# A three-stage float32 kernel on one TensorE: other PSUM banks for half of an output phase, a later place for operand preparation, and another slot for weight conversions

## The chip, the cores and the metric

The kernel runs on one core of a Trainium2 chip. The metric is the time of one execution on the device in microseconds (us). The core's engines work side by side, each through its own list of instructions in order: TensorE (PE in the profile: matrix products into the PSUM banks), VectorE (DVE: arithmetic on tiles), ScalarE (ACT: copies, casts, activation functions) and SyncE (SP: it issues the transfers of the DMA queues). An instruction that needs another engine's result waits for it, and everything behind it on its engine waits too.

## What is computed

The reference, cut to what matters:

```
# attention over a window of 64 positions, 4 batches x 8 heads, 576 positions, head size 64
mask = (rel >= 0) & (rel < 64);  attn = softmax(where(mask, q @ k.T / 8, -1e9)) @ v
x = attn.transpose(0, 2, 1, 3).reshape(2304, 512)
# gated MLP, d_ff = 1536
xn = x / sqrt(mean(x * x, axis=-1) + 1e-6) * rms_g
x2 = (silu(xn @ w_gate) * (xn @ w_val)) @ w_out
# second MLP, d_ff = 2048
h = x2 @ w_in
out = (h * sigmoid(1.702 * h)) @ w_out2
```

All is float32. The kernel gets float32 accuracy from three fast products: an operand is split into a high part (rounded to the fast matmul format) and a low part (the remainder), and high x high, low x high and high x low are summed in PSUM. In the code these are the pairs `xh`/`xl`, `ah`/`al`, `whi`/`wlo`.

## The kernel before

The 2304 tokens are columns of the matmuls, features are the partitions. There are eight PSUM banks: four accumulators with the tags `acc0` to `acc3`, two with the tags `g` and `v`, and a pool `atp` of two with the tag `att`. There are three passes.

**Pass one** (to about 366 us of the span) takes six blocks `j` of 384 tokens through the first half of the gated MLP's features, six chunks `f` of 128. One chunk is 36 matmuls of 128x384: twelve into `psg` (L95, the gate), twelve into `psv` (the value), and twelve of `emit_O` that add the chunk before into the four `acc` banks. ACT takes a function of the gate (L803), DVE multiplies (L806, L810), ACT and DVE split the result into `ah` and `al` (L813, L814). Between the matmuls of block `j` the attention of block `j+1` is worked off, pinned in program order on PE: scores `ps_s` (32 small matmuls), their mask and row maximum on DVE (eight L380 for a group of 128 tokens), the exponentials on ACT (L392), the sums, transposes (`ps_t`), and `ps_v`, the product with v. The scores of one group fill one bank of four tiles; `ps_v` is put into a bank of the same pool and so comes after L380s that read it. At the end of the last chunk of a block `split_x` makes the next block's `xh` (ACT L494 and DVE L492, two each) and `xl` (four L496 on DVE) from the scaled attention output; the next block's first `psg` needs `xh`, its ninth to twelfth matmul need `xl`.

**Weight conversions.** The weights come in another 32-bit format and are converted by `w_step`: two passes on ACT (L230, L231), a shift and an addition on DVE (L232, L237). For pass two a conversion is finished by the next `w_step` call, which runs `w_products`: four additions on DVE (L172 to L175), the high part on ACT (L180) and the low part on DVE (L181, 128x1792), and two stores to DRAM. In pass one a conversion is called from `extras(f, i)`, three slots per chunk, with `s = 3 * f + i`. In the blocks after the first it is called where `s % 9 == 8`: twice in a block, after `f=2` and after `f=5`, the latter at the end of the block. Conversions for pass two go on until block 3.

**Operand preparation.** Pass two multiplies by a scheme of seven products in place of eight (on halves of tokens and features), whose operands `xop` are sums and differences of the input tiles `xr`, split in high and low. `x_steps` returns seven steps for a superblock: a sum on DVE (L661, in four of them), the high part on ACT (L663), the low part on DVE (L664). For the first superblock the steps are called in the last block of pass one, one after chunk 1 and two after each later chunk, and they are needed when pass two begins.

**Pass two** (366 to 587 us) is the second half of the gated MLP's features, in three superblocks of 768 tokens. Each has six chains of seven products (`psa`, `psb`; even chains in the banks `g` and `v`, odd ones in the two `att` banks) and then an output phase, `out_units`. This is made of two halves, `t=1` and then `t=0` (384 tokens each). A half is four units of twelve matmuls (three per accumulator) and four closing pieces `last(t, c)` of six matmuls, 72 in all. A closing piece is followed by L919 on DVE, which adds the partial result of pass one (loaded by L918) to the accumulator `c`, and by a store (L920). Both halves use `acc0` to `acc3`, so a first matmul of `t=0` into `acc` number `c` waits for the L919 of `t=1` with that `c`. The closing pieces of `t=0` are spread over the first chain of the next superblock. On DVE the last seven `xop` steps for the next superblock, a weight conversion and the products `g` (L880, L883) lie around that place.

**Pass three** (587 us to the end) is the second MLP with the same product scheme for `w_in` and plain products for `w_out2`.

The order on the engines is made by the code order, by a scheduler that moves instructions by their readiness, by `keep_in_program_order` on PE, and by `issue_after`, which puts an instruction behind a given one.

Of the kernel before, what the change touches and what calls it, by code (L numbers as in the profile page):

```python
# [8 lines left out]
F32 = mybir.dt.float32  # L9
# [4 lines left out]
ALU = mybir.AluOpType  # L14
# [8 lines left out]
def window_attention__gated_mlp__mlp_kernel(  # L23
# [13 lines left out]
    nc = tc.nc  # L37
# [4 lines left out]
    KC = DM // 128  # L42
# [21 lines left out]
    acc_p = ctx.enter_context(tc.tile_pool(name="acc", bufs=1, space=PSUM))  # L64
# [4 lines left out]
    atp = ctx.enter_context(tc.tile_pool(name="atp", bufs=2, space=PSUM))  # L69
# [87 lines left out]
    def after(ins):  # L157
        return tc.issue_after(ins) if ins is not None else nullcontext()
# [326 lines left out]
    def rms_scale(x, sq, lo, hi, s4=None):  # L485
        rms_sum(x, sq, lo, hi, s4)
        return rms_spread(x, lo, hi)

    def split_x(x, xh, xl, T):
        for c in range(KC):  # L490
            if c % 2:
                nc.vector.tensor_copy(xh[:, c, :T], x[:, c, :T])  # L492
            else:
                last = nc.scalar.copy(xh[:, c, :T], x[:, c, :T]).ins  # L494
        for c in range(KC):
            nc.vector.tensor_tensor(xl[:, c, :T], x[:, c, :T], xh[:, c, :T].bitcast(F32), ALU.subtract)  # L496
        return last

    def proj(ps, w, xh, xl, T):
# [16 lines left out]
    xd = {}  # L516
# [54 lines left out]
    for m in range(2 * m0, N_ATT):  # L571
        b, i = divmod(m, m0)
        t, n = score_at[m - 2 * m0], score_at[m - 2 * m0 + 1] - score_at[m - 2 * m0]
# [13 lines left out]
    if True:  # L587
# [27 lines left out]
        x, sq = x_of(0)  # L615
# [21 lines left out]
        T = TB  # L637
# [8 lines left out]
        def x_raws(src):  # L646
            r = [wp.tile([128, KC, TB], F32, tag="w", name="xr") for _ in range(2)]
            for e in range(2):
                nc.sync.dma_start(out=r[e], in_=src(e))
            return r  # L650

        def x_steps(r, ops):
            a11, a12, a21, a22 = r[0][:, 0:2, :], r[0][:, 2:4, :], r[1][:, 0:2, :], r[1][:, 2:4, :]
            subs = [
                (0, None, a11), (6, (a21, a11, a21, ALU.subtract), a21), (5, (a21, a22, a21, ALU.subtract), a21),
                (4, (a11, a11, a21, ALU.add), a11), (2, (a21, a12, a21, ALU.subtract), a21), (1, None, a12), (3, None, a22),
            ]

            def step(i, total, src):
                if total:  # L660
                    nc.vector.tensor_tensor(*total)  # L661
                t = x1p.tile([128, 2, 2, TB], F32R, tag="xop", name="xop")
                nc.scalar.copy(t[:, 0], src)  # L663
                nc.vector.tensor_tensor(t[:, 1], src, t[:, 0].bitcast(F32), ALU.subtract)  # L664
                ops[i] = t

            return [lambda a=a: step(*a) for a in subs]
# [100 lines left out]
        for j in range(NB):  # L768
# [17 lines left out]
            def extras(f, i):  # L786
                s = 3 * f + i
                for fn in slots.pop(j * NS + s, ()):
                    fn()
                if j == 0:  # L790
                    if s % 2 == 0:
                        w_step(n_wh)
                elif s % 9 == 8:
                    w_step(n_w1)

            pend = None
            for f in range(FH):
# [17 lines left out]
                if f == FH - 1 and not end:  # L815
                    nxh = xp.tile([128, KC, TB], F32R, tag="x", name="xh")
                    nxl = xp.tile([128, KC, TB], F32R, tag="x", name="xl")
                    x = xs.pop(j + 1)[0]
# [12 lines left out]
                if f == 0 and end:  # L831
                    at_es.close()
                    x1p = ctx.enter_context(tc.tile_pool(name="x1p", bufs=7))
                    ops = {}
                    todo = x_steps(x_raws(lambda e: xd[e]), ops)
                if f == 4 and end:
                    loads(0, 2)
                if f >= 1 and end:
# [54 lines left out]
        def out_units(sb, g):  # L893
# [13 lines left out]

            def unit(t, k):
                if k == 0:
                    accs[t] = [acc_p.tile([128, 512], F32, tag=f"acc{c}", name="acc") for c in range(KC)]  # L910
                for c in range(KC):
                    mms(t, *order[k], c)

# [280 lines left out]
```

## Time and profile before

| what | value |
|---|---|
| time, median of 3 runs (lowest, highest) | 953.79 us (949.55, 954.65) |
| profiled execution: its time | 956.72 us |
| its span | 954.9 us |
| PE busy | 919.3 us, 96% |
| DVE busy | 605.9 us, 63% |
| ACT busy | 512.1 us, 54% |
| mean granted TensorE clock | 0.979 of full speed |

The span is the profiled execution from its first to its last instruction; 1.8 us of the time lie around it. Busy is the time in which an engine had an instruction under way. Matmuls overlap, so that a train of 128x384 ones starts one every 0.174 us where each has a duration of about 0.34 us; the end of a train therefore hangs over the next start by about 0.17 us, and the idle time that a row gives is shorter than the delay of the start by about that much. "Issue" as a releaser is a wait for which the profile shows no releasing instruction.

### The profile page before, as it was taken

Reading aid. Unit: us, or ns where it says so; the run is one execution under the profiler, and the core shown is the slowest. Engines: PE = TensorE matmul, PEld = TensorE weight load, DVE = VectorE, ACT = ScalarE, POOL = GpSimd, SP = SyncE. Lnnn points to the kernel's source line nnn. Section 1 sums busy time; section 2 is a strip of 40 time slices with the busy share of each in tenths; the row PEclk is TensorE's granted clock in tenths of the full one; section 3 lists DMA queues with packets and bytes.
Section 4 is the critical chain, followed back from the end, with each engine's and each line's share of the span. In section 5 each row is a group of like instructions: output and inputs, shape, how many; then the busy total and the mean of one; then the engine's idle time right before and its main releaser. Section 6 shows DMA issues by size and latency. Waiting matters only on the chain.

```text
span 954.9 us, 16476 instructions
## 1 busy us (share of the span) xinstructions
PE 919.3 (96%) x6398; PEld 880.5 (92%) x6398; DVE 605.9 (63%) x1216; ACT 512.1 (54%) x1028; POOL 12.1 (1%) x39
## 2 busy tenths in 40 slices
PE   8889899999989899989999999999999999999998
PEld 7888798998989899979999999988989999999998
DVE  5798477667774725892892787656563469334753
ACT  7796475655653416742651664665554555345442
POOL 2000000000000000000000000000000000000000
PEclk9899799999999999989998999999999999999999
DMA  9865555675753274977976999988667778867861
GB/s 224 228 181 169 132 143 169 179 210 186 210 160 140 104 276 156 340 267 263 370 274 209 336 366 323 332 279 325 233 244 281 272 301 282 297 216 273 321 226 50
DMA packets 153646, 227.96 MB, mean 239 GB/s; under 512 B 80608, under 2 KB 130784, under 8 KB 149984
## 3 DMA queue, kind: packets, MB, share of 16 engines
q1 hardware_dynamic: 153040, 226.91, 71.1%
q8 instruction: 50, 0.82, 0.3%
q14 instruction: 28, 0.23, 0.1%
q10 hardware_dynamic: 528, 0.00, 0.0%
HBM read 167.64 MB, written 59.24 MB: 238 GB/s over the span
## 4 chain that ended last, share of the span: by engine, by line
PE 74%; DVE 12%; ACT 5%; DMA 5%; issue 3%; SPq 0%; POOL 0%; DVEq 0%; ACTq 0%
PE acc L95 17%; PE psa L95 14%; PE psb L95 11%; PE psg L95 7%; PE psv L95 7%; PE acca L95 6%; PE accb L95 5%; DVE xop L664 2%; PE ps_v L95 2%; PE ps_s L95 2%; PE ps_t L95 1%; DMA xr<-x 1%; ACT st L231 1%; DMA st<-in_moe_w_in_dram 1%; DVE xr L661 1%
## 5 line engine op out<-in xcount | busy, mean ns | idle before, releaser
L95 PE MATMUL psa<-xop,wt 128*128 128x384 f32 x1008 | 192.9, 335 | 0.4 <-DMA wt<-wv 0.4
L95 PEld LDWEIGHTS psa<-xop,wt 128*128 128x128 f32 x1008 | 176.6, 188 | 3.3 <-DMA wt<-wv 0.8
L95 PE MATMUL psb<-xop,wt 128*128 128x384 f32 x756 | 147.1, 335 | 0.8 <-DVE sn L704 0.8
L95 PEld LDWEIGHTS psb<-xop,wt 128*128 128x128 f32 x756 | 132.6, 188 | 3.3 <-DVE sn L704 1.1
L704 DVE TENSOR_TENSOR sn<-sn,psb 128x384 f32<-128x384 f32 x84 | 46.3, 552 | 80.5 <-PE psb L95 79.6
L95 PE MATMUL acc<-g,w 128*128 128x384 f32 x432 | 87.5, 356 | 6.2 <-DVE part L919 5.9
L95 PEld LDWEIGHTS acc<-g,w 128*128 128x128 f32 x432 | 80.9, 202 | 9.9 <-DVE part L919 9.2
L95 PE MATMUL psg<-xh,w 128*128 128x384 f32 x288 | 68.5, 363 | 4.6 <-ACT xh L494 2.6
L95 PE MATMUL acca<-wo,sop 128*128 128x256 f32 x576 | 72.0, 283 | 0.2 <-DVE sop L1002 0.2
L1002 DVE TENSOR_TENSOR sop<-g,sop 128x768 fp32r<-128x768 f32 x56 | 53.3, 957 | 28.6 <-ACT sop L1001 28.5
L95 PEld LDWEIGHTS acca<-wo,sop 128*128 128x128 f32 x576 | 70.8, 191 | 0.5 <-DVE sop L1002 0.5
L700 ACT COPY sn<-psa 128x384 f32<-128x384 f32 x84 | 40.0, 476 | 57.3 <-PE psa L95 57.3
L1001 ACT CAST sop<-g 128x768 fp32r<-128x768 f32 x56 | 46.4, 835 | 40.5 <-PE accb L95 23.2
L95 PE MATMUL acc<-whi,g 128*128 128x512 f32 x192 | 67.8, 392 | 0.0
L392 ACT ACTIVATE p<-p,sm 128x128 f32<-128x128 f32 x128 | 49.6, 389 | 22.2 <-DVE sm L380 22.1
L95 PE MATMUL psv<-xh,w 128*128 128x384 f32 x288 | 61.2, 344 | 0.0
L95 PEld LDWEIGHTS psg<-xh,w 128*128 128x128 f32 x288 | 51.5, 198 | 8.3 <-ACT xh L494 3.6
L95 PE MATMUL acc<-ah,w 128*128 128x384 f32 x288 | 58.9, 340 | 0.0
L978 ACT ACTIVATE g<-sn 128x384 f32<-128x384 f32 x48 | 25.2, 526 | 52.3 <-DVE sn L704 52.3
L95 PE MATMUL accb<-wo,sop 128*128 128x256 f32 x432 | 52.8, 283 | 0.0
L95 PEld LDWEIGHTS accb<-wo,sop 128*128 128x128 f32 x432 | 52.3, 192 | 0.0
L95 PEld LDWEIGHTS psv<-xh,w 128*128 128x128 f32 x288 | 50.8, 191 | 0.4 <-issue 0.2
(135 smaller groups left out, 1514.8 us busy)
## 6 DMA issues: line engine op xcount, KB each, us to landing
wt<-wh SPq DMA_DIRECT2D x48, 896.0 KB, 6.4
wo<-wp SPq DMA_DIRECT2D x28, 1024.0 KB, 6.1
st<-in_moe_w_out_dram SPq DMA_DIRECT2D x28, 512.0 KB, 7.8
wt<-wg SPq DMA_DIRECT2D x14, 896.0 KB, 6.6
wt<-wv SPq DMA_DIRECT2D x14, 896.0 KB, 8.0
xr<-x SPq DMA_DIRECT2D x12, 768.0 KB, 7.3
wh<-whi SPq DMA_DIRECT2D x8, 896.0 KB, 8.3
wh<-m SPq DMA_DIRECT2D x8, 896.0 KB, 8.6
```

The source lines that it names most:

```text
L95: ins = op(*args, **kw)
L231: nc.scalar.activation(lo, lo.bitcast(U32), AF.Copy, scale=2.0 ** -29)
L392: last_exp[0] = nc.scalar.activation(p[e][:, hp, :], p[e][:, hp, :], AF.Exp, bias=sm[:, 0, i:i + 1], scale=-1.0, accum_out=sm[:, 1, i:i + ...
L661: nc.vector.tensor_tensor(*total)
L664: nc.vector.tensor_tensor(t[:, 1], src, t[:, 0].bitcast(F32), ALU.subtract)
L700: nc.scalar.copy(t, ps[:, :TB])
L704: nc.vector.tensor_tensor(t, t, ps[:, :TB], ALU.add)
L978: hold[0] = nc.scalar.activation(g[pg, q][:, j % 2], c, AF.Gelu_apprx_sigmoid).ins
L1001: nc.scalar.copy(t[:, 0], src)
L1002: nc.vector.tensor_tensor(t[:, 1], src, t[:, 0].bitcast(F32), ALU.subtract)
```

## The change

The change has three parts. (1) In `out_units` the four accumulators of `t=0` are now two `att` banks and `acc0`, `acc1`, in this order; `t=1` keeps `acc0` to `acc3`. (2) The steps of `x_steps` for the first superblock get `hold_on=split_end`: each instruction of a step is put behind the last L496 of the latest `split_x` on the same engine. That is an order on DVE alone, where the L496 stands. (3) The conversions in the blocks after the first are called at `s % 9 == 4`, in the middle of chunks 1 and 4 (behind the value's products, `i=1`), instead of at the end of chunks 2 and 5.

```
     def split_x(x, xh, xl, T):
...
         for c in range(KC):
-            nc.vector.tensor_tensor(xl[:, c, :T], x[:, c, :T], xh[:, c, :T].bitcast(F32), ALU.subtract)
+            low = nc.vector.tensor_tensor(xl[:, c, :T], x[:, c, :T], xh[:, c, :T].bitcast(F32), ALU.subtract).ins
+        split_end[0] = low
         return last
...
-        def x_steps(r, ops):
+        def x_steps(r, ops, hold_on=()):
...
             def step(i, total, src):
+                with ExitStack() as es:
+                    for ins in hold_on:
+                        es.enter_context(after(ins))
+                    make(i, total, src)
+
+            def make(i, total, src):
                 if total:
                     nc.vector.tensor_tensor(*total)
...
-                elif s % 9 == 8:
+                elif s % 9 == 4:
                     w_step(n_w1)
...
-                    todo = x_steps(x_raws(lambda e: xd[e]), ops)
+                    todo = x_steps(x_raws(lambda e: xd[e]), ops, split_end)
...
             def unit(t, k):
                 if k == 0:
-                    accs[t] = [acc_p.tile([128, 512], F32, tag=f"acc{c}", name="acc") for c in range(KC)]
+                    tags = ("acc0", "acc1", "acc2", "acc3") if t else ("att", "att", "acc0", "acc1")
+                    accs[t] = [
+                        (atp if tag == "att" else acc_p).tile([128, 512], F32, tag=tag, name="acc") for tag in tags
+                    ]
```

The order of the instructions on PE is the same in both kernels; the waits differ. On PE at the first superblock's output phase, where the half `t=0` begins, there stood before (acc_4604 is the last accumulator of `t=1`, acc_4751 to acc_4754 are those of `t=0` for `c` = 0 to 3, the name in brackets is the semaphore that is waited for):

```order
L95 MATMUL acc_4604<-g_4625,w_4426 128x384 x3
L95 MATMUL acc_4751<-g_4330,w_4250 128x384 [waits DVE_49]
L95 MATMUL acc_4751<-g_4330,w_4250 128x384 x2
L95 MATMUL acc_4752<-g_4330,w_4250 128x384 [waits DVE_49]
L95 MATMUL acc_4752<-g_4330,w_4250 128x384 x2
L95 MATMUL acc_4753<-g_4330,w_4250 128x384 [waits DVE_49]
L95 MATMUL acc_4753<-g_4330,w_4250 128x384 x2
L95 MATMUL acc_4754<-g_4330,w_4250 128x384 [waits DVE_49]
L95 MATMUL acc_4754<-g_4330,w_4250 128x384 x2
```

and in the changed kernel, at the same place on PE:

```order
L95 MATMUL acc_4604<-g_4625,w_4426 128x384 x3
L95 MATMUL acc_4751<-g_4330,w_4250 128x384 x3
L95 MATMUL acc_4752<-g_4330,w_4250 128x384 x3
L95 MATMUL acc_4753<-g_4330,w_4250 128x384 [waits DVE_49]
L95 MATMUL acc_4753<-g_4330,w_4250 128x384 x2
L95 MATMUL acc_4754<-g_4330,w_4250 128x384 [waits DVE_49]
L95 MATMUL acc_4754<-g_4330,w_4250 128x384 x2
```

The first two accumulators have no wait any more, and the last two wait for the L919 of the first two accumulators of `t=1`.

On DVE around the `split_x` for the last block of pass one (L492 and L496; L661 and L664 are the operand preparation) there stood before:

```order
L661 TENSOR_TENSOR xr<-xr 128x768
L810 TENSOR_TENSOR a<-a,psv 128x384
L661 TENSOR_TENSOR xr<-xr 128x768
L664 TENSOR_TENSOR xop<-xr,xop 128x768
L814 TENSOR_TENSOR al<-a,ah 128x384
L492 CAST xh<-xraw 128x384 x2
L496 TENSOR_TENSOR xl<-xraw,xh 128x384 x2
L661 TENSOR_TENSOR xr<-xr 128x768
L664 TENSOR_TENSOR xop<-xr,xop 128x768
L496 TENSOR_TENSOR xl<-xraw,xh 128x384 x2
```

and in the changed kernel (its line numbers are higher by 2 in `split_x` and by 9 behind it):

```order
L819 TENSOR_TENSOR a<-a,psv 128x384
L823 TENSOR_TENSOR al<-a,ah 128x384
L494 CAST xh<-xraw 128x384 x2
L498 TENSOR_TENSOR xl<-xraw,xh 128x384 x4
L673 TENSOR_TENSOR xop<-xr,xop 128x768
L670 TENSOR_TENSOR xr<-xr 128x768
```

All of the preparation on DVE now stands behind the split, whose four L498 follow each other.

On DVE in block 1 of pass one, ahead of the L380s of one of its score groups, there stood before:

```order
L453 TENSOR_TENSOR sq<-s_1699 128x128
L814 TENSOR_TENSOR al<-a,ah 128x384
L806 SCALAR_TENSOR_TENSOR a<-a,psg 128x384
L380 ISA p,sm<-ps_s,masks 128x128
L380 ISA sm 128x1
```

and in the changed kernel:

```order
L453 TENSOR_TENSOR sq<-s_1699 128x128
L823 TENSOR_TENSOR al<-a,ah 128x384
L815 SCALAR_TENSOR_TENSOR a<-a,psg 128x384
L232 TENSOR_SCALAR m<-st 128x1024
L237 ISA m<-st,m 128x2048
L380 ISA p,sm<-ps_s,masks 128x128
L380 ISA sm 128x1
```

The second conversion of this block, which stood at its end, now has its shift and addition ahead of these L380s.

## Rows read from the trace of the kernel before

**Rows 1.** The page's first part: busy time, share of the span, instructions.

```profile
PE 919.3 (96%) x6398; PEld 880.5 (92%) x6398; DVE 605.9 (63%) x1216; ACT 512.1 (54%) x1028; POOL 12.1 (1%) x39
```

**Rows 2.** PE's waits: what waited for whom, us in total, times, longest.

```profile
PE acc L95 <- DVE part L919: 5.9, 6, 1.8
PE ps_v L95 <- issue: 5.5, 4, 2.6
```

**Rows 3.** Timeline, PE, first superblock's output phase: start, us, instruction, [idle before <- releaser].

```profile
414.80 7.06 PE L95 MATMUL acc<-g,w 128*128 128x384 f32 x36
423.68 1.01 PE L95 MATMUL acc<-g,w 128*128 128x384 f32 x3 [1.82 <-DVE part L919]
425.08 2.66 PE L95 MATMUL acc<-g,w 128*128 128x384 f32 x6 [0.39 <-DVE part L919]
428.62 9.65 PE L95 MATMUL acc<-g,w 128*128 128x384 f32 x39 [0.87 <-DVE part L919]
```

**Rows 4.** Timeline, DVE, the same stretch.

```profile
416.54 0.55 DVE L880 TENSOR_TENSOR a<-a,psa 128x384 f32<-128x384 f32 x1
...
423.07 0.55 DVE L919 TENSOR_TENSOR part<-part,acc 128x384 f32<-128x384 f32 x1
```

**Rows 5.** Timeline, PE, second superblock's output phase.

```profile
500.16 1.72 PE L95 MATMUL acc<-g,w 128*128 128x384 f32 x6 [1.05 <-DVE part L919]
503.29 9.82 PE L95 MATMUL acc<-g,w 128*128 128x384 f32 x39 [1.41 <-DVE part L919]
```

**Rows 6.** Windows: stretch, length, busy times of PE to POOL, granted clock, DMA share, GB/s.

```profile
219.27:222.69 3.42, 3.37 (x37) 3.19 (x38) 2.84 (x14) 3.42 (x15) 0.00 (x0) 0.50 0.10 24
424.07:434.31 10.24, 8.98 (x27) 7.45 (x26) 7.95 (x13) 1.69 (x1) 0.00 (x0) 0.50 1.00 344
502.58:509.41 6.83, 6.12 (x19) 6.12 (x20) 1.53 (x3) 0.00 (x0) 0.00 (x0) 0.50 0.88 283
```

**Rows 7.** Timeline, PE, pass one: stalls at the starts of blocks 2 to 5.

```profile
161.60 0.44 PE L95 MATMUL psg<-xh,w 128*128 128x384 f32 x1 [1.38 <-ACT xh L494]
...
164.30 0.45 PE L95 MATMUL psg<-xl,w 128*128 128x384 f32 x1 [0.32 <-DVE xl L496]
...
219.32 1.98 PE L95 MATMUL ps_v<-pt,qkv 128*64 128x64 f32 x32 [2.21 <-issue]
...
275.36 1.15 PE L95 MATMUL ps_v<-pt,qkv 128*64 128x64 f32 x32 [2.56 <-issue]
...
323.05 1.49 PE L95 MATMUL psg<-xh,w 128*128 128x384 f32 x7 [0.81 <-DVE xh L492]
...
326.45 0.91 PE L95 MATMUL psg<-xl,w 128*128 128x384 f32 x3 [1.75 <-DVE xl L496]
```

**Rows 8.** Timeline, DVE, inside the last `split_x` of pass one.

```profile
324.11 0.95 DVE L661 TENSOR_TENSOR xr<-xr 128x768 f32<-128x768 f32 x1
```

**Rows 9.** Instruction groups by line and shape: count, busy us, mean ns, idle before.

```profile
L237 DVE CUSTOM_DVE_ANT_0 m<-st,m 128x2048 uint16<-128x2048 uint16 x34 | 41.5, 1221 | 3.5 <-ACT st L231 2.8
L231 ACT ACTIVATE st<-st 128x1024 int32<-128x1024 uint32 x34 | 39.3, 1155 | 0.0
L181 DVE TENSOR_TENSOR m<-m,whi 128x1792 fp32r<-128x1792 f32 x14 | 28.3, 2023 | 4.6 <-ACT whi L180 4.4
L230 ACT ACTIVATE st<-st 128x1024 f32<-128x1024 f32 x25 | 28.2, 1130 | 3.2 <-DMA st<-in_moe_w_in_dram 2.4 <-DMA st<-in_moe_w_out_dram 0.9
L232 DVE TENSOR_SCALAR m<-st 128x1024 uint32<-128x1024 uint32 x34 | 23.5, 692 | 16.7 <-ACT st L230 15.8 <-DMA qkv<-in_q_dram 0.5 <-ACT st L228 0.4
L172 DVE TENSOR_TENSOR m<-m 128x256 f32<-128x256 f32 x22 | 9.2, 419 | 0.0
```

**Rows 10.** Timelines, block 1: ACT's gate function, a score group's L380s, the `ps_v` behind.

```profile
144.22 0.49 ACT L803 ACTIVATE a<-psg 128x384 f32<-128x384 f32 x1 [1.47 <-PE psg L95]
...
145.96 0.29 DVE L380 CUSTOM_DVE_ANT_0 p<-ps_s,masks 128x128 f32<-128x128 f32 x1 [0.67 <-PE ps_s L95]
...
147.78 1.15 PE L95 MATMUL ps_v<-pt,qkv 128*64 128x64 f32 x32
```

More of the change, by code (lines that the diff above doesn't have):

```diff
@@ L487, in rms_scale @@
         return rms_spread(x, lo, hi)
+    split_end = [None]
     def split_x(x, xh, xl, T):
```

## The prediction

> **What bounds the kernel now.** First the busy times: TensorE is busy for 96% of the span, the next engine for 63% [rows 1]. So a change counts only where it lets TensorE start earlier or run faster, and what there is to win lies in its stalls and in stretches at half clock. Second its waits by releaser: the largest is on L919, the evictions of the output phase, with 5.9 us in six waits, and the next a wait of `ps_v` without a named releaser, 5.5 us in four [rows 2]. The places of both, read next in the timelines, are where this change works: the middle of the output phases [rows 3, 5] and the starts of the blocks of pass one [rows 7]. Third the granted clock: 2.4 GHz nearly everywhere, but at the lower level, 1.2 GHz (0.50), for 10.24 us behind the first stall of L919, for 6.83 us around the second, and for 3.42 us from the `ps_v` stall at 219.32 [rows 6]. It did not fall at every stall: at 275.36 TensorE had idled 2.56 us, and the 32 matmuls of `ps_v` behind took 1.15 us, against 1.98 at 219.32 [rows 7]. The pitch of a 128x384 matmul at full clock is 0.174 us (39 of them take 6.79), and a stall delays the next start by about 0.2 us more than its idle time, since a train hangs over.
>
> **Part 1, other banks.** In the first superblock the half `t=1` ends with 36 matmuls from 414.80 that last 7.06 us; less the overhang of 0.17 the next could start at 421.69. The first one of `t=0` starts at 423.68, its second accumulator at 425.08, its fourth at 428.62, each behind an L919 [rows 3]. The L919 themselves are late because VectorE works off its list in order: the first starts at 423.07 [rows 4], although its accumulator was complete before. The change does not move these evictions. But now `c`=0 and 1 go to the `att` banks, last read by L880 at 416.54 [rows 4], and so run at once, from 421.69 to 422.73. `c`=2 takes the bank of the first L919 and starts at 423.68 as `c`=0 did (a delay of 0.95), `c`=3 that of the second, and starts at 425.08 in place of 428.62. Then 39 matmuls without a wait follow; they took until 428.62 + 9.65 less 0.17 = 438.10, for the most part at half clock [rows 3, 6]. At full clock they end at 425.08 + 6.79 = 431.87: **6.2 us earlier**, 3.5 of it from the start and 2.7 from the clock.
>
> In the second superblock the stalls are at 500.16 and 503.29 [rows 5]; the release that `c`=3 now needs is the one that let `c`=1 go at 500.16. So 500.16 + 6.79 = 506.95, against 503.29 + 9.82 less 0.17 = 512.94: **6.0 us**. In the third superblock there is one short wait, 5.9 less the five shown (5.54) [rows 2, 3, 5], below 0.4. In the order of the changed kernel two `wlo` conversions of VectorE lie ahead of all four L919 there, so that I count nothing. Costs: the first `att` bank is wanted again by the next superblock's second chain, which starts only when the first chain and the closing pieces of `t=0` between its products are over, and `c`=0 is evicted first among these; I count nothing, and at most one L919 of 0.55 [rows 4] per superblock if that fails.
>
> **Part 2, preparation held.** At the last block's start TensorE waits 0.81 for an `xh` of VectorE and 1.75 for an `xl` [rows 7]; inside the split stands an L661 (324.11, 0.95 us) [rows 8], with an L664 of like length behind it, and more of both lie close ahead. With all of these behind the split the four `xl` follow each other and both waits go: 0.81 + 1.75 and the overhang of two stalls, **3.0 us**. The preparation itself is wanted at 366. The seven steps are eleven instructions of this length on VectorE, 10.5 us between the block's own work: done by about 340, so that some 25 us of the last block cover them. Were that cover gone, each step late would cost an L661 and an L664, 1.9 us.
>
> **Part 3, conversions at another slot.** What leaves the block ends: a conversion is 0.69 + 1.22 us on VectorE, its completion 4 x 0.42 and 2.02 more, 5.6 in all, and on ScalarE 1.13 + 1.16 lie ahead of it [rows 9]. At the start of block 2 it lay in front of the split: TensorE idles 1.38 ahead of 161.60, 0.32 at 164.30 [rows 7], and there are two more gaps of this size; each with its overhang, 1.55 + 3 x 0.49, 3.0 us. In block 3 the `ps_v` at 219.32 had waited 2.21 for L380s that stood behind an L237, an L172, an L174 and the split. The conversion's part is 1.22 + 2 x 0.42 = 2.06 at the most and nothing at the least, where the split is held by other things than VectorE; the L814 ahead of the split needs the last chunk's products, so that I take 0.8. With it goes the clock's fall: half of 3.42 [rows 6], 1.7, which I count since the stall is then shorter by a third. In block 4 the `ps_v` at 275.36 waits 2.56 [rows 7] behind the same row of instructions; between 0 and 2.06 again I take 1.8, since there a part of the split already lies between the L380s. Together 3.0 + 0.8 + 1.7 + 1.8 = **7.3 us**.
>
> What comes into the blocks' middle: in block 1 the two conversions now have their additions on VectorE ahead of the L380s of two score groups. The worked case is the second: its L380s start at 145.96, right when the scores are there, and the `ps_v` behind them at 147.78 [rows 10]. Now ScalarE does L230 and L231 first (from 144.71, when its gate function ends [rows 10], to 147.0), then L237 takes until 148.2, and the fourth L380, four starts of some 0.21 later, lets `ps_v` go at 149.05: 1.3 us lost. The first costs 0.95 at `ps_k` by the same count, and the later links of both chains (sums and scaling behind L181) another 0.95, of which 0.4 comes back at a wait that was there before: **2.8 us**. In blocks 2 and 3 the additions of the moved conversions fall between score groups; I count 0. The bounds: nothing, if the scheduler's place is met by an idle engine, and up to 5.6 us for each of six conversions, all of it on the score chain. I take 2.8, since the row at 145.96 shows a chain with no slack to its `ps_v`, and only block 1 has L237 right ahead of L380s.
>
> **The sum.** -6.2 - 6.0 - 3.0 - 7.3 + 2.8 = **-19.7 us**. Against the profiled execution of 956.72 (its span and 1.8 around it) that is 937.0; this execution lies 2.9 above the median of 953.79, so for a median I predict **934 us** (-2.1%). A measurement of this kernel can tell about 0.5% from no change: faster means below 949.0, slower above 958.6.
>
> **The rivals.** *The clock falls all the same.* TensorE keeps idling 0.78 and some 0.7 in the first superblock and 1.05 in the second, and the fall at 502.58 came with one stall of 1.05 over and the next, 1.41, under way [rows 5, 6]. Against it: 2.56 at 275.36 brought no fall [rows 7]. Where both stretches stay, half of 10.24 + 6.83 is given back, 8.5: 942.5; with the first alone, 939. The Trainium skill ("TensorE: Matmul & The Clock Gate", the section on psum-queue depth-cycling) describes this side: a kernel that cycles its banks each iteration idles a little between groups of matmuls, and its clock swings between both levels. By this the times just given would hold; the trace shows both outcomes.
>
> *The conversions cost what they return.* If block 1's count holds in blocks 2 and 3 too (three blocks at about 2.5 to 3), 7.3 is gone: 941.5. For it: the chain at 145.96 has no slack; against: the order there.
>
> *The banks bring nothing.* The data rate is 344 and 283 GB/s in the two half-clock stretches, with the transfer engines busy for 1.00 and 0.88 of them [rows 6]; a TensorE that comes 6 us earlier to the next superblock may wait there for weights or partial results in place of L919. Then 12.2 is lost: 946. Against it: none of TensorE's large waits is for a transfer [rows 2]. The Trainium skill has a case of this kind ("TensorE: Matmul & The Clock Gate", section on HAM oscillation): adding double buffering in PSUM gave no further gain once the matmuls ran in one piece. Here they do not run in one piece [rows 3], so that I give it little.
>
> *Slower.* All six moved conversions stand fully on the score chain, which paces pass one: six times 5.6 is 33.6, and three stretches like the one of 6.83 [rows 6] at half clock behind new stalls, 10; less the 19.7 + 2.8 of gains, +21: 975. The point from which it decides is a cost of 22.5 / 6 = 3.75 us per conversion; the worked one costs 1.3 to 2. For it only that `ps_v` waits are the second largest already [rows 2].
>
> *It does not do what it says*, the waits move without a gain: 953.8. The order of instructions speaks against it, since the two waits are gone.
>
> **How the numbers follow.** Forecast 0.55, the clock 0.15, the conversions' cost 0.11, the banks 0.05, slower 0.06, nothing 0.08. Faster is the first four, 0.86; same 0.08; slower 0.06. Range: the forecast's own bounds are 929 (no cost of the conversions and 2 us of ends not counted) and 939; it reaches over the clock and the conversions' cost to 946, at the banks' case, and leaves out the slower case and the unmoved one. 929 to 946.
>
> **What would show it.** In the output phases the rows after `t=1` should show two idle gaps of below 1 us, then 39 matmuls in 6.9 us; the stretch of 0.50 gone at both. At the last block's start the two psg gaps are gone. At 161 and 219 the gaps shrink or go; `ps_v` and `ps_k` of block 1 show new waits of about 1 us. A PE wait for DMA of several us at the next superblock, or new gaps of `ps_v` in blocks 2 and 3, would make the prediction wrong.

## The result, and the profile after

| what | before | changed |
|---|---|---|
| time, median (lowest, highest) | 952.2 us (949.55, 954.65), 4 runs | 936.87 us (935.7, 938.94), 4 runs |
| ratio | | 0.9842, 95% interval 0.9804 to 0.9879 |
| profiled execution: time, span | 956.72, 954.9 us | 935.7, 933.9 us |
| mean granted TensorE clock of it | 0.979 | 0.991 |

The change makes the kernel 1.6% faster, about 15 us; 934 was forecast. A later set of runs on another occasion gave 939.3 against 952.23, ratio 0.9859 (0.9832 to 0.9885). The two profiled executions lie 21.0 us apart, more than the medians, so there are two things to explain: where the 21.0 come from, and why the medians differ by less.

The page's busy times of the changed kernel (engine, us, share of the span, instructions), then TensorE's waits (who waited <- for whom: us, times, longest). They answer to [rows 1] and [rows 2]; L931 is now the eviction that was L919.

```profile
PE 908.9 (97%) x6398; PEld 871.4 (93%) x6398; DVE 604.4 (65%) x1216; ACT 512.7 (55%) x1028; POOL 13.4 (1%) x39
```

```profile
PE ps_v L95 <- issue: 2.9, 4, 1.2
...
PE acc L95 <- DVE part L931: 1.3, 2, 0.7
...
PE ps_k L95 <- issue: 0.7, 1, 0.7
...
PE acc L95 <- DVE g L892: 0.3, 1, 0.3
```

The evictions' waits fell from 5.9 us in six to 1.3 in two, those of `ps_v` from 5.5 to 2.9. A wait of `ps_k` is new. The timeline of TensorE in the output phase of the first superblock (start, us, instruction, [idle before <- releaser]; to be read beside [rows 3]):

```profile
406.46 3.12 PE L95 MATMUL acc<-g,w 128*128 128x384 f32 x17
409.89 4.61 PE L95 MATMUL acc<-g,w 128*128 128x384 f32 x25 [0.31 <-DVE g L892]
415.16 0.80 PE L95 MATMUL acc<-g,w 128*128 128x384 f32 x3 [0.66 <-DVE part L931]
416.57 7.03 PE L95 MATMUL acc<-g,w 128*128 128x384 f32 x39 [0.60 <-DVE part L931]
423.44 1.20 PE L95 MATMUL psa<-xop,wt 128*128 128x384 f32 x6
```

and in that of the second, which answers to [rows 5] (two views, the first of which ends at 487, so that its 53 matmuls reach into the second's 39):

```profile
477.88 9.43 PE L95 MATMUL acc<-g,w 128*128 128x384 f32 x53
```

```profile
485.68 7.00 PE L95 MATMUL acc<-g,w 128*128 128x384 f32 x39
492.52 1.20 PE L95 MATMUL psa<-xop,wt 128*128 128x384 f32 x6
```

The 25 matmuls from 409.89 are the last 19 of `t=1` and, without a gap, the six of `c`=0 and 1. Then come two short waits, and 39 matmuls in 7.03 us where there were 9.65. In the second superblock the trains follow each other without a wait. In windows over the two phases (stretch, length, busy times of PE, PEld, DVE, ACT and POOL, granted clock, DMA share, GB/s), of the changed kernel:

```profile
409.00:429.00 20.00, 18.43 (x104) 17.46 (x103) 14.50 (x20) 8.09 (x11) 0.00 (x0) 1.00 0.89 308
479.00:497.00 18.00, 18.00 (x105) 17.90 (x104) 11.26 (x18) 5.69 (x8) 0.00 (x0) 1.00 0.75 271
```

The clock is 2.4 GHz throughout; the stretches at 1.2 GHz of [rows 6] are gone. In pass one, beside [rows 7] and [rows 10]:

```profile
120.97 0.63 PE L95 MATMUL ps_k<-ident,qkv 128*128 128x128 f32 x4 [0.65 <-issue]
...
147.85 1.15 PE L95 MATMUL ps_v<-pt,qkv 128*64 128x64 f32 x32 [1.16 <-issue]
...
156.56 0.94 PE L95 MATMUL ps_r<-ident,ry 128*128 128x128 f32 x6 [0.34 <-POOL ry L469]
...
161.20 1.96 PE L95 MATMUL psg<-xh,w 128*128 128x384 f32 x8
...
217.35 1.15 PE L95 MATMUL ps_v<-pt,qkv 128*64 128x64 f32 x32 [1.07 <-issue]
...
270.29 1.15 PE L95 MATMUL ps_v<-pt,qkv 128*64 128x64 f32 x32 [0.29 <-issue]
...
316.50 1.66 PE L95 MATMUL psg<-xh,w 128*128 128x384 f32 x8
317.99 1.23 PE L95 MATMUL psg<-xl,w 128*128 128x384 f32 x4
```

Block 2 starts without a wait that the row names (161.20), the `ps_v` of blocks 3 and 4 wait 1.07 and 0.29 in place of 2.21 and 2.56, the 32 of block 3 take 1.15 us and not 1.98, and block 5 starts without a gap. The first three rows (`ps_k`, `ps_v` and `ps_r`) are what the new slot costs in block 1.

Since TensorE's order is the same in both kernels, matmul by matmul the starts can be subtracted. Changed less before: -1.6 at 110, -0.8 at 120.97, +0.07 at 147.85, +0.8 at 156.56 (block 1 has lost 2.4 on balance, with 0.4 won between), -1.4 at 166.67 (block 2 has won 2.2), -3.4 at 222, -5.1 at 270.29, -8.1 at 318.31, -14.7 at 423.44, -20.4 at 492.52, -21.0 at the end. So 1.6 us of it was there at 110, ahead of all that the change touches: the profile of the kernel before has 20.5 us at half clock ahead of 110, that of the changed kernel 17.1, and half of this difference is 1.7. The rest, 19.4 us, is to be set against the sum of 19.7: 3.4 from 110 to the end of block 4 (part 3), 3.1 at the start of block 5 (part 2), 6.3 and 5.8 in the two output phases (part 1), and 0.8 elsewhere.

### The profile page after: what moved, and what is told of

It is laid out like the page before. It is cut to its first block, busy times and chain, and to the rows that moved or that the text cites. A ratio compares the mean times of both kernels' runs of the same rounds, so it can differ in the third digit from the quotient of the medians.

```text
span 933.9 us, 16476 instructions
## 1 busy us (share of the span) xinstructions
PE 908.9 (97%) x6398; PEld 871.4 (93%) x6398; DVE 604.4 (65%) x1216; ACT 512.7 (55%) x1028; POOL 13.4 (1%) x39
## 4 chain that ended last, share of the span: by engine, by line
PE 76%; DVE 10%; DMA 5%; ACT 4%; issue 2%; SPq 2%; POOL 1%; DVEq 0%; ACTq 0%
PE acc L95 18%; PE psa L95 15%; PE psb L95 11%; PE psg L95 8%; PE psv L95 7%; PE acca L95 6%; PE accb L95 5%; PE ps_v L95 2%; PE ps_s L95 1%; DMA xr<-x 1%; PE ps_t L95 1%; SPq L296 1%; ACT st L231 1%; DMA st<-in_moe_w_in_dram 1%; DVE xop L673 1%
## 5 line engine op out<-in xcount | busy, mean ns | idle before, releaser
L95 PE MATMUL acc<-g,w 128*128 128x384 f32 x432 | 79.0, 335 | 1.6 <-DVE part L931 1.3
L95 PEld LDWEIGHTS acc<-g,w 128*128 128x128 f32 x432 | 75.0, 188 | 2.7 <-DVE part L931 1.9
L180 ACT CAST whi<-m 128x1792 fp32r<-128x1792 f32 (+1 forms) x22 | 39.0, 1770 | 22.2 <-DVE m L175 22.2
```

The lines of the kernel that those rows point to most:

```text
L95: ins = op(*args, **kw)
L180: nc.scalar.copy(hi, m)
```

## Experiments

### One part at a time

Each part alone in the kernel before, and all three once more, timed together. The edits are the three pieces of the diff above; for the first, for instance, only

```
-                    accs[t] = [acc_p.tile([128, 512], F32, tag=f"acc{c}", name="acc") for c in range(KC)]
+                    tags = ("acc0", "acc1", "acc2", "acc3") if t else ("att", "att", "acc0", "acc1")
...
```

> Part 1 alone: the kernel before with the half t=0 in the banks att, att, acc0, acc1. Theory (the stalls behind L919 and the half clock they bring are the cost, 6.2 us at the first superblock and 6.0 at the second, and nothing else of the change touches them): about 12 us faster than before, 940 on the median of 952, idle gaps on L919 of 0.5 to 1 us each and no stretch at 0.50 in the output phases; pass one unchanged, with its stalls at block starts. Rival (gains of the parts depend on each other, since an earlier or later TensorE only moves the clock's falls): 4 to 8 us, with a half-clock stretch left in one of the two places.

> Part 2 alone: the operand preparation on VectorE behind the last split, old banks, old slot. Theory: 3.0 us, all of it at the start of the last block of pass one (the gaps of 0.81 and 1.75 at psg gone): 949 on 952. Rival (the preparation comes late and pass two waits for xop, or VectorE's list fills up behind the split): 0 or slower, with a wait of psa or psb at the start of pass two.

> Part 3 alone: the conversions at s % 9 == 4. Theory: 7.3 us back at the starts of blocks 2 to 4, 2.8 us lost in block 1 at ps_k and ps_v of two score groups: 4.5 us faster, 947.5 on 952. Rival (the conversion costs in the middle of a block what it cost at its end): within 1 us of before.

> All three parts, the changed kernel once more beside the single parts. Theory (the parts lie at different places and add up): the sum of what the three single runs gain, 15 to 20 us, 932 to 937 on 952. Rival (they overlap): less than the largest two of them together.

| kernel | median, us | ratio to before (952.23 us) | 95% interval |
|---|---|---|---|
| banks alone | 945.19 | 0.9919 | 0.9893 to 0.9945 |
| preparation alone | 950.4 | 0.9964 | 0.9941 to 0.9986 |
| slot alone | 948.64 | 0.9966 | 0.9947 to 0.9985 |
| all three | 939.3 | 0.9859 | 0.9832 to 0.9885 |

By the ratios the parts gain 7.7, 3.4 and 3.2 us, 14.3 together; all three at once gain 13.4, and 15.0 in the first set of runs (0.9842). So they add up within their intervals. The rival that they overlap, with less than the 11.1 of the largest two, lies at the very edge of the interval of all three (11.0 to 16.0). The preparation and the slot lie where they were expected (3.0 and 4.5). The banks alone give 7 to 8 us, with an interval of 5.2 to 10.2 that leaves out the 12 of the sum. And yet the profile of the banks alone is as the theory says, with two short waits and no more on the evictions:

```profile
PE psa L95 <- DMA wt<-wv: 1.6, 2, 1.1
PE acc L95 <- DVE part L922: 1.3, 2, 0.7
```

The first row is new. In the output phase of this kernel the same 39 matmuls behind the last eviction take 7.06 us. What is missing on the median has to come either from the kernel before (its profile was worse than most executions) or from something behind the output phase (the wait for `wt`). Both are seen below. Start by start against the profile of the kernel before, the banks alone win 6.3 us in the first output phase and 5.9 in the second, and lose 2.2 between them, most of it at the two waits for `wt`.

### How much half clock the kernel before has

> The kernel before once more, for another profile of its output phases. Theory (the stalls behind L919 are fixed, the half clock behind them varies between executions, so that the profile that the sum was made from held more of it than most): the same stalls within 0.2 us, a half-clock stretch of another length at the two places, in all below the 17.1 us of the first profile. Rival (the profile was typical, and the banks gain less for another reason): again about 17 us at half clock.

> The same kernel a third time, with the same two readings: below 17.1 us at half clock in the two output phases, or about 17 again.

With the preparation and the slot alone, which leave the old banks in place, there are four more profiles of the old output phases. Windows of 20 and 18 us over the two phases, one fence for each kernel: first the kernel before (its first profile), then its two repeats, the preparation alone, the slot alone. The column to read is the granted clock, third from the end.

```profile
420.00:440.00 20.00, 16.92 (x70) 15.07 (x69) 12.02 (x17) 5.03 (x7) 0.00 (x0) 0.74 1.01 370
496.00:514.00 18.00, 15.39 (x70) 14.44 (x70) 8.11 (x11) 2.53 (x4) 0.00 (x0) 0.81 0.79 291
```

```profile
417.00:437.00 20.00, 16.73 (x70) 15.04 (x69) 12.19 (x17) 5.13 (x8) 0.00 (x0) 0.74 1.01 373
493.00:511.00 18.00, 15.40 (x79) 14.44 (x78) 8.38 (x13) 3.25 (x6) 0.00 (x0) 0.91 0.82 292
```

```profile
420.00:440.00 20.00, 17.00 (x71) 15.16 (x70) 11.89 (x17) 4.90 (x7) 0.00 (x0) 0.74 1.01 372
496.00:514.00 18.00, 15.40 (x70) 14.44 (x69) 7.95 (x11) 2.37 (x4) 0.00 (x0) 0.81 0.83 292
```

```profile
416.00:436.00 20.00, 16.73 (x70) 15.05 (x69) 12.30 (x17) 5.11 (x8) 0.00 (x0) 0.74 1.01 367
492.00:510.00 18.00, 15.41 (x79) 14.45 (x78) 8.50 (x12) 3.40 (x6) 0.00 (x0) 0.91 0.81 292
```

```profile
417.00:437.00 20.00, 16.29 (x74) 14.82 (x73) 12.15 (x18) 4.95 (x7) 0.00 (x0) 0.83 1.02 372
493.00:511.00 18.00, 15.41 (x86) 14.45 (x85) 8.16 (x12) 2.99 (x5) 0.00 (x0) 1.00 0.83 302
```

The length at half clock is twice (1 - clock) times the window: 17.2, 13.6, 17.2, 13.6 and 6.8 us. In the second superblock the stalls are the same in all five, 1.05 and 1.41 us, so the same stall is followed by a fall of the clock in one execution and by none in another: with the slot alone the second phase has the stalls and a clock of 1.00. The 39 matmuls behind the second stall, in the first repeat and in the slot alone, to be set beside the 9.82 us of [rows 5]:

```profile
500.54 8.32 PE L95 MATMUL acc<-g,w 128*128 128x384 f32 x39 [1.41 <-DVE part L919]
```

```profile
499.79 7.05 PE L95 MATMUL acc<-g,w 128*128 128x384 f32 x39 [1.41 <-DVE part L919]
```

So the half clock is worth 2.8, 1.3, 2.8, 1.3 and 0 us there in the five, and 2.1 to 2.7 in the first superblock, whose 39 matmuls take 9.13 to 9.74 us. The two repeats disagree as to the forecast, one below 17.1 and one at it: the profile that the sum was made from is at the upper end of what is seen, but no freak.

The clock of every execution says more. Over 47 executions of the kernel before the mean clock runs from 0.977 to 0.989 with a median of 0.984; turned into us at half clock (twice (1 - clock) times the time) that is 21 to 44 with a median of 30.5, and a straight line through the 47 gives time = 940.0 us + 0.41 times the us at half clock, with a correlation of 0.92. The profiled execution with 0.979 has 40 us: by that line it lies 3.9 us above the median one through the clock alone. Start by start it lies 4.1 us behind its first repeat, whose 0.984 is the median clock: 1.8 of this are there at 110, 1.5 come behind the `ps_v` stall at 219.32, where the repeat has no half clock, 1.5 in the second output phase, and 0.7 are won back elsewhere. All executions of the changed kernel have 0.988 to 0.991, a median of 16.9 us; of the banks alone 22.7. By the same line the 13.6 us less at half clock are worth some 5.6 us, an estimate; the rest of the gain is shorter stalls, less the new waits.

### The place of the wait

The changed kernel with the two `att` banks at the end of `t=0`:

```
-                    tags = ("acc0", "acc1", "acc2", "acc3") if t else ("att", "att", "acc0", "acc1")
+                    tags = ("acc0", "acc1", "acc2", "acc3") if t else ("acc0", "acc1", "att", "att")
```

> The changed kernel with the two att banks at the end of t=0 in place of its beginning: acc0, acc1, att, att. The same banks and the same two L919 to wait for, but TensorE now waits in one piece at c=0 (some 1.7 us in the first superblock, 1 us in the second) and has nine more matmuls to do behind the last wait instead of ahead of it. Theory (a stall costs its own length, and a longer one brings back the half clock in some executions): 1 us later at each of two superblocks, and up to 2 to 5 us more where a half-clock stretch follows; 2 to 7 us slower than the changed kernel, ratio to before about 0.988 to 0.993. Rival (only the number of banks counts, the place of the wait does not): the same as the changed kernel, 0.985.

938.77 us, ratio 0.9858 (0.983 to 0.9887). The changed kernel itself was not timed beside this version and those below, so that they are compared with it by their ratios to the kernel before. TensorE's timeline of the first superblock:

```profile
409.59 3.57 PE L95 MATMUL acc<-g,w 128*128 128x384 f32 x19 [0.30 <-DVE g L892]
414.86 0.80 PE L95 MATMUL acc<-g,w 128*128 128x384 f32 x3 [1.70 <-DVE part L931]
416.26 3.91 PE L95 MATMUL acc<-g,w 128*128 128x384 f32 x21 [0.60 <-DVE part L931]
```

The longer wait is in one piece as expected, and the start-by-start difference to the changed kernel grows by 1.0 us here and by 1.25 in the second superblock, the 1 us each that was expected. On the median this cannot be told from the changed kernel: the trace speaks for the theory's lower end, the time alone leaves the rival standing. Its profile has no half-clock stretch in the output phases, even behind 1.70 us idle here and 1.05 in the second superblock: the upper end of the theory, that one longer stall brings the fall back, is not borne out by this one profile.

### The conversions: places on the score chain

The changed kernel with its conversions at slots meant to leave no additions ahead of L380s:

```
-                elif s % 9 == 4:
+                elif s in ((2, 11) if j == 1 else (2, 13)):
```

> The changed kernel with the conversions at slots 2 and 11 in block 1 and 2 and 13 in the later blocks, where their additions on VectorE do not stand ahead of a score group's L380s. Theory (the middle of block 1 costs 2.3 to 2.8 us since L237 delays those L380s): the new waits of ps_k and ps_v in block 1 go, the block starts stay as they are in the changed kernel, 2 to 3 us faster than it, ratio about 0.982. Rival (any place in the block costs the same, the scores only hide one wait behind another): the same as the changed kernel, 0.985.

943.81 us, ratio 0.9906 (0.9877 to 0.9934): slower than the changed kernel (its fastest execution, 941.14, lies above the slowest of the changed kernel, 940.18), against both readings. TensorE's timeline in block 1 has

```profile
145.10 1.09 PE L95 MATMUL ps_t<-ident,p 128*128 128x128 f32 x4 [3.43 <-DVE p L404]
145.84 1.31 PE L95 MATMUL acc<-al,w 128*128 128x384 f32 x3
146.94 1.06 PE L95 MATMUL ps_t<-ident,p 128*128 128x128 f32 x4
147.65 2.91 PE L95 MATMUL psg<-xh,w 128*128 128x384 f32 x8
```

and VectorE just before

```profile
138.59 0.68 DVE L232 TENSOR_SCALAR m<-st 128x1024 uint32<-128x1024 uint32 x1
139.98 1.23 DVE L237 CUSTOM_DVE_ANT_0 m<-st,m 128x2048 uint16<-128x2048 uint16 x1 [0.70 <-ACT st L231]
141.12 0.55 DVE L819 TENSOR_TENSOR a<-a,psv 128x384 f32<-128x384 f32 x1
141.59 0.16 DVE L402 TENSOR_SCALAR sm<-sm 128x8 f32<-128x8 f32 x1
...
143.74 1.22 DVE L404 TENSOR_TENSOR p<-p,sm 128x1024 f32<-128x1024 f32 x1
```

The conversion now stands between the L380s and the scaling of the same group (L402 to L404). `ps_t`, which transposes the scaled scores, waits 3.43 us, and eight `psg` matmuls behind it take 2.91 us, at half clock. Start by start against the changed kernel this profile, the slowest of the six executions, loses 4.6 us in block 1 and 1.3 in block 2, the latter at a `ps_t` again, with a conversion and four additions between its L380s and its L404. A wait for `wt` costs 3.5 more (see below), and 1.7 were there at 110. Nor did the edit clear the place ahead of the L380s: at the first score group of block 1 the additions of a completion and an L181 of 2.02 us stand there, and the `ps_k` behind waits 1.11 us in place of 0.65. So this kernel does not test the theory at that row. The thought was too narrow as well: the place between the L380s and L404 costs more than the one ahead of the L380s. That every place on the chain scores, L380, L404, `ps_t`, `ps_v` is dear where TensorE has no other work left is a reading of these two places, not shown for the others.

The conversions at their old slot, each instruction behind the last split:

```
-                elif s % 9 == 4:
-                    w_step(n_w1)
+                elif s % 9 == 8:
+                    with after(split_end[0]):
+                        w_step(n_w1)
```

> The changed kernel with the conversions at their old slot (s % 9 == 8), but each of their instructions behind the last L496 of the latest split on its engine. Theory (two things cost at a block's start: the additions ahead of the split, and those ahead of the L380s of the first score group behind it): the psg stall at the start of block 2 goes, as in the changed kernel, but ps_v at the starts of blocks 2 to 4 waits 2 to 4 us behind conversions that have piled up; about 4 to 8 us slower than the changed kernel, ratio 0.99 to 0.994. Rival (only the split counts): the same as the changed kernel, 0.985.

942.97 us, ratio 0.9895 (0.9862 to 0.9928), about 4 us slower than the changed kernel, at the theory's lower end. Start by start against the changed kernel it wins 2.7 us in block 1 (0.8, 1.2 and 0.5 at the three rows shown above), and loses 2.2 at the start of block 2 and some 5 in blocks 3 and 4, where TensorE's timeline has

```profile
217.68 1.15 PE L95 MATMUL ps_v<-pt,qkv 128*64 128x64 f32 x32 [2.34 <-issue]
```

```profile
273.58 1.25 PE L95 MATMUL ps_v<-pt,qkv 128*64 128x64 f32 x32 [2.74 <-issue]
```

In front of the first of these rows VectorE has an L172, an L174 and an L232 between the split and the L380s. So a free split is only one half of the slot's gain; the other is a first score group whose L380s have no conversion ahead of them.

If block 1 is where the new slot costs, it should have none:

```
-                elif s % 9 == 4:
+                elif j > 1 and s % 9 == 4:
```

> The changed kernel with no conversions in block 1: the six for pass two are called at the slot of the change in blocks 2, 3 and 4 in place of 1, 2 and 3. Theory (the two conversions in block 1 cost 2.8 us on its score chains, and the attention chain of a later block has more room): the waits of ps_k and ps_v in block 1 and the start of block 2 free, 2 to 3 us faster than the changed kernel if block 4 takes its two for nothing, up to 1.5 lost there; ratio about 0.982. Rival (each block's chain is equally tight, the cost only moves to block 4): the same as the changed kernel, 0.985. A third reading (weights come later to pass two and wt waits grow): slower than the changed kernel.

935.71 us (933.5 to 938.1), ratio 0.9828 (0.9799 to 0.9856). In block 1 the two rows that answer to 120.97 and 147.85 are now

```profile
120.63 0.60 PE L95 MATMUL ps_k<-ident,qkv 128*128 128x128 f32 x4
```

```profile
146.15 1.15 PE L95 MATMUL ps_v<-pt,qkv 128*64 128x64 f32 x32
```

without a wait, and the start-by-start difference to the changed kernel moves by -3.0 us over block 1, and by +0.6 in block 4. That is the cost of block 1 measured by itself. A wait for `wt` takes 1.2 of it back in this profile. This is the fastest version of the study; by the ratios it gains 1.3 to 3 us on the changed kernel, and the intervals overlap, so that on the time alone the gain is likely, not sure.

### The new wait for weights

The profile of all three parts together has what that of the changed kernel has not (TensorE, second superblock's chains):

```profile
464.76 3.46 PE L95 MATMUL psa<-xop,wt 128*128 128x384 f32 x10 [2.32 <-DMA wt<-wv]
```

This `wt` was issued at 453.45 and landed 11.3 us later; in the changed kernel's profile its counterpart took 9.0 us and held TensorE up by 0.2, and in the kernel before it took 7.8 us. TensorE does not come to it sooner: without the wait it would reach it 8.8 us after the issue in this kernel, in the changed one and in all five profiles with the old banks, where the landing took 7.7 to 8.7 us. It is the transfer that takes longer with the new banks, 8.1 to 11.3 us where the load stands at this place of the queue. Why it does is open. The stretch of 24 us ahead has the transfer engines busy throughout, here in the kernel with all three parts (the DMA share is 1.00 in the kernel before too, at 364 GB/s):

```profile
440.00:464.00 24.00, 22.44 (x130) 22.11 (x128) 20.88 (x39) 16.42 (x27) 0.00 (x0) 1.00 0.99 379
```

The ten matmuls behind the wait take 3.46 us where twelve take 2.24 elsewhere: the clock has fallen there, and the wait costs 3.7 us with it. That is most of the 4.5 us between this profile and that of the changed kernel; 1.4 more were there at 110, and 0.6 is won back elsewhere. The experiment moved one conversion of the second superblock to a later place:

```
-                put(t0 + 2.5 + (8 if sb == 0 else 14) * k, lambda: w_step(n_wi))
+                put(t0 + 2.5 + (8 if sb == 0 else 14) * k + (6 if sb == 1 and k == 1 else 0), lambda: w_step(n_wi))
```

> The changed kernel with one conversion of the second superblock of pass two six places later, so that three loads of raw weights (st) stand behind two loads of wt in the queue of SyncE, and a store of 896 KB further back. Theory (the bank part gained less on the median than in its profile because a TensorE that is earlier meets a wt that lands 9 to 11 us after its issue, 2.3 us of waiting in one profile of the changed kernel and 1.1 in that of the banks alone): wt lands sooner, no wait of psa for wt in the second superblock, 1 to 3 us faster than the changed kernel, ratio about 0.982, with less spread. Rival (that wait was chance): the same as the changed kernel, 0.985, or the loads wait elsewhere.

939.27 us, ratio 0.9857 (0.9832 to 0.9882), no gain. In its profile this `wt` lands after 6.4 us and is not waited for, but another wait has come in the same superblock:

```profile
462.83 1.33 PE L95 MATMUL psb<-xop,wt 128*128 128x384 f32 x6 [1.35 <-ACT sn L709]
```

The moved conversion's work on ScalarE delays the copy of a product there. The load was eased and the time went elsewhere, as the rival had it. How often the wait for `wt` falls in a timed execution is not known: in the second superblock it is 2.3, 2.0, 1.6, 1.2 and 0.5 us in five of the eight profiles with the new banks and below 0.1 in three, and none of the five with the old banks has it there. (In the third superblock profiles of both kinds have one, of at most 0.5.)

## Why the prediction was right, and where it was not

**The bound.** Right: TensorE is at 97% after the change as at 96% before, its time is given by its stalls and its clock, and these are where the gain came from.

**Part 1.** In the profile the steps hold. `c`=0 and 1 run at once, `c`=2 and 3 wait for the first two evictions, and 39 matmuls go through at full clock. Against the first of the last 36 matmuls of `t=1` (414.80 in [rows 3], 406.46 after), 8.35 us early, the next superblock is 14.7 early (438.10 and 423.44): 6.3 us, 6.2 forecast. From there to the end of the second phase (512.94 and 492.52, 20.4 early) 5.8, 6.0 forecast. In the first phase the stalls are 0.66 and 0.60, 0.78 and some 0.7 by forecast. In the second the stall of 1.05 that the rival on the clock counts did not appear, and by the prediction's own rows it could not: the six matmuls of `c`=0 and 1, 1.04 us, now run in that time. The start of `c`=3 it had right, 500.16, which is 485.86 at the 14.3 us that the changed kernel is ahead there; 485.68 came. The wait of 0.31 for an L892 costs nothing: the kernel before is delayed by as much at the same place, inside its train of 36. For the third superblock nothing was counted; it won 1.4, of which 0.6 at a `wt` that the kernel before waits for, and gave back 0.6.

On the median it is wrong by size. The step that failed is the term of the clock in the sum: 2.7 of the 6.2 us, 2.9 of the 6.0 and the 1.7 of block 3 were taken from one execution as though every execution had them. In the five profiles with the old banks the first is 2.1 to 2.7 and the second 2.8, 1.3, 2.8, 1.3 and 0; in the first repeat, whose time and clock are the median ones, the second is 1.3 and the third is nothing.

Subtracting 2.9 us for the profile's distance from the median did not put this right. It took part of the same time off twice, since of the 4.1 us between that profile and the repeat only the 1.8 ahead of 110 lie where the change wins nothing; the prediction's list of stretches at half clock leaves out those ahead of 110, 20.5 us of that profile. The same sum from the repeat, 952.62 less 19.7 and with 1.5 us given back at each of the two places, is 935.9, an estimate. That 934 lies as near as it does is in part luck: the gain was 3 us too large for a typical execution, and the median of three runs that it was taken from, 953.79, lies 1.2 above that of the 47.

What is left to 936.87 and 939.3, 1 to 3.4 us, is of the size of the new wait for `wt`: 0.5 to 2.3 us idle in five of eight profiles, 3.7 with the clock in one. That is the mechanism of the rival "the banks bring nothing", at a third of its price or less. How much of the rest it makes in the timed executions is not shown. Banks alone: 7 to 8 us and not 12.2.

**Part 2.** Right: 3.0 forecast, 3.1 start by start at the two gaps of block 5 (1.3 and 1.8), 3.1 again in the profile of the preparation alone, 3.4 by the ratio with an interval of 1.3 to 5.6. VectorE's timeline of the changed kernel there:

```profile
316.23 0.62 DVE L494 CAST xh<-xraw 128x384 fp32r<-128x384 f32 x2
316.77 1.96 DVE L498 TENSOR_TENSOR xl<-xraw,xh 128x384 fp32r<-128x384 f32 x4
318.64 0.95 DVE L673 TENSOR_TENSOR xop<-xr,xop 128x768 fp32r<-128x768 f32 x1
```

The four L498 follow each other, the preparation comes behind them, and no wait for `xop` appeared in pass two.

**Part 3.** Block 2: 3.0 forecast, 2.2 came. Block 3: 0.8 and 1.7 forecast, 1.1 and 1.5 came. Block 4: 1.8 forecast, 1.9 came. Block 1: 2.8 lost by forecast, 2.4 in the trace, and 3.0 won when it was taken out by itself. In all the part brings 3.4 us in the trace and 3.2 by its ratio, 4.5 forecast. The worked case was `ps_v` at 149.05, against 147.78; the trace has it 1.23 us later than its surroundings, 1.3 forecast. The reason given, additions ahead of the L380s, is right for these two rows (at the `ps_k` three additions of the completion stand there too, behind the L237) but not the general rule: the kernel with slots 2 and 11 shows that the place behind the L380s costs more. "Nothing in blocks 2 and 3" holds within 0.5 us.

**The rivals.** The clock did not fall in the output phases of any of the eight profiles with the new banks. In seven of them the stalls on the evictions are at most 0.73 us, so that the rival's case of 1.05 did not arise; the one with the `att` banks at the end had 1.70 and 1.05, and its clock did not fall either. The Trainium skill's case of a kernel that cycles banks and swings between the two clocks ("TensorE: Matmul & The Clock Gate", the section on psum-queue depth-cycling) did not come about here: both windows after the change have 1.00. Its other case, no further gain from double buffering in PSUM (same page, section on HAM oscillation), did not either: the banks alone give 0.8%. The conversions' cost did not spread to blocks 2 and 3 as that rival had it. The slower case did not come; the dearest slot tried is still faster than the kernel before.

## What to carry to other kernels

If half of an accumulation waits for the evictions of the other half, look for banks that are idle in just that stretch, and give them to the accumulators that start first. When a sum is made from one profile, count the stalls in full, but the half clock behind them only as far as several executions show it: the clock of each timed run tells whether the profiled one was typical. Where the sum counts such a clock term as won, the profile's distance from the median must not be taken off a second time. A background task on a busy engine is best put in the block whose critical chain has most room; here leaving block 1 out was worth 3.0 us in the trace and 1 to 3 on the median, and the one other slot tried within it cost more.

## What was not expected of the hardware

The same stall does or does not bring a fall of the clock from one execution to the next: 1.05 and 1.41 us of idle time in the second output phase were followed by 6.8, 3.4, 6.8, 3.4 and 0 us at half clock in five executions, of three kernels that have the same instructions there on TensorE. The spread of the kernel before (948.5 to 957.7 us) goes along with this clock to a correlation of 0.92. And a transfer of 896 KB that landed 7.7 to 8.7 us after its issue in the five profiles with the old banks took 9.0 and 11.3 us in two executions of the changed kernel, with the transfer engines busy all the time, as in the kernel before. TensorE wants it 8.8 us after the issue in either kernel, so that before the change 0.1 to 1.1 us were to spare.
